# A delta-rule attention with an MLP on one core: constants and a weight request moved within the opening, chunk 0's output turned earlier

## The chip, the cores and the metric

The kernel runs on one core of one Trainium2 chip. The time is device microseconds of one launch. Engines in the profile: PE is TensorE's matrix multiply (PEld its weight loads), DVE is VectorE, ACT is ScalarE, POOL is GpSimd, SP is SyncE, which only issues transfers. Each engine runs its own queue in order, and the queues meet only at semaphores.

## The reference

Attention by the delta rule over 4 batches x 8 heads, 768 steps, head size 48, and then an MLP on all 3072 tokens (384 to 2048 to 384 with a tanh GELU).

```python
k_n = k / (np.linalg.norm(k, axis=-1, keepdims=True) + 1e-06)
state = np.zeros((B, H, D, D), dtype=np.float32)
for t in range(S):
    y[:, :, t] = np.einsum('bhd,bhde->bhe', q[:, :, t], state)
    v_old = np.einsum('bhde,bhd->bhe', state, kt)
    state = state + bt[:, :, :, None] * np.einsum('bhd,bhe->bhde', kt, vt - v_old)
...
h = x @ w_in
g = 0.5 * h * (1.0 + np.tanh(c * (h + 0.044715 * h * h * h)))
return (g @ w_out).astype(np.float32)
```

## The kernel before

The 768 steps are cut into 12 chunks of 64. A chunk covers all 32 heads; it is worked as two units of 16 heads each (unit u = 2 x chunk + 0 or 1). Inputs are float32, the working copies bf16. What one chunk goes through:

- **norms** (L497 to L503): squares of k on ACT (`sq`), their sums on DVE (`sum`), the root (`pow`, on ACT for the first three chunks), `eps` and the reciprocal `inv`.
- **prep** (L531 to L586): `kn` multiplies k by the inverse norm into the tile `tok`, `qb` casts q beside it; PE turns them (`Tk`, `Tq`, or `T` for both, L540), an eviction `kTk`, `kTq` or `kT` follows; Gram products `GD`, `GQ` or `G` (L564); `dn` evicts the k-k half, `wq` the masked k-q half.
- **leaf** (L633 to L669): `F` folds the 8 x 8 blocks on the diagonal, `lp`, `x0` and six pairs `xm`, `xa` on DVE solve them, `xb` scales by beta.
- **scale** (L599 to L623): `xe` or `xec` spread that into the tile `zt`; `KZ` and `GM` are products on PE, `kz` and `lw` their evictions. `lw` holds the lower triangle of the chunk's matrix.
- **invert** (L682 to L717): `X10`, `X11` copy its diagonal into `bd`, and two doublings (`A4`, `rt4`, `B4`, `bde4..`, then `A5`, `rt5`, `B5`, `be5..`) give the inverse.
- **chain** (L752 to L812): from chunk to chunk, `V`, `K`, `R`, `U`, `Un`, the new state `S` and `Sn`, the output `O` and `On`; the output is turned for the MLP by `X` on PE and the eviction `xT`, or by a transposing transfer.
- **mlp** (L824 to L844): 16 up-projections `up`, GELU in four parts on ACT, 8 groups of `down` matmuls, `Z` evicts, `out` stores.

A name such as `GM.4` is GM of unit 4, `X.0` is X of chunk 0. Nothing is scheduled at run time or by a planner: the text `ORDER` lists every operation once, in one global order. `kn.2:d` means kn of unit 2 on DVE (a is ACT, g POOL, s SP), no letter means PE, and `@6` is the first PSUM bank of the result. From this list each engine gets its own queue. `Flow.add` records what each operation reads and writes, and `Flow.emit` sets a semaphore wait wherever an operation needs one on another engine, or a bank whose last reader is on another engine. So an operation that waits holds all that stands behind it in its engine's queue.

Constants come in the same list. Some names: `tmpl`, a template of -1 diagonals; `sel`, `rows`, `blk`, `own`, masks for the leaf; `rowz` clears `rows` and `rows1` (L382) fills it; `two` (L380), `unit`, `muq`, `mlw`, `low1` more masks; `pad` and `bdz` clear borders of `tok` and `bd`; `triwq`, `trilw` preset `wq`, `lw` from the template; `ladj4`, `ladj5` (L416, L418) preset the tiles `rl`; `first` (L400) sets the first column of `xl`; `wz` clears the operand of filler matmuls (`fill`, L426). `betaN` evict the turned beta; `w1.0`, `w1.1` (L481) request the two halves of W1 on POOL's queue, `w2` those of W2. The loads of q, k and v (L472) are on SP's queue, the first few of k on ACT's.

The lines that set one of the waits that matter below, the bank of a product:

```python
            if o.alloc:
                b = self.at[o.alloc[0]]
                for y in range(b, b + o.alloc[1]):
                    o.bankdeps.update(last[y])
```

Of the kernel before, what the change touches and what calls it, by code (L numbers as in the profile page):

```python
# [15 lines left out]

ORDER = """
bdz3:d tmplz:g k0x1.10:a k1.01:s tmpl0:g tmpl1:g bdz5:d k0x1.00:a beta11:s blk1:g one:g pad2:g pad0:d pad5:d ident:g trilw0:d beta01:s beta10:a bdz4:d
ident2:g bdz0:g k0x1.01:s k0x1.11:a mmlw:d identf:d blk2:g k1.00:s beta00:a blk3:g k0x0.00:a k1.10:s half:g own:g triwq4:g trilw1:a k1.11:s sel:d
q0.10:s k0x0.10:a unit:d betaT1@0 triwq0:g q0.01:s mmuq:d mln0:g tabS:a bdz2:g sq.0b:a k2.00:s pad4:g mwp0:g betaN101:d k0x0.11:a betaT0@6 sum.0b:d  # L20
rowz:g q0.00:s betaN100:d mln1:g pow.0b:a q0.11:s eps.0b:d pad1:g inv.0b:d betaN001:d sq.1:a kn.1:g q2.11:s k0x0.01:a sum.1:d k2.10:s muq0:g Tk.1@1
muq1:g ladj4.0:a k2.01:s betaN011:d pow.1:a betaN110:d eps.1:g pad3:d k2.11:s inv.1:d triwq1:d betaN010:d low1:d kn.2:d v0.10:s kn.3:d qb.1:a Tk.2@7
v0.01:s qb.0:g Tk.3@5 kTk.2:d q2.01:s rows1:g Tq.1@4 sq.0a:a betaN111:d kTk.1:d q2.10:s kTq.1:d kTk.3:a sum.0a:d q2.00:s GD.3@4 betaH1:d pow.0a:a
Tq.0@7 sq.2:a eps.0a:d rpad0:g v1.00:s inv.0a:d GD.2@2 betaN000:d GD.1@0 dn.3:a kn.0:g betaL1:d q1.01:s betaH0:d betaS1@6 dn.2:a sum.2:d low2:g
q1.00:s dn.1:a Tk.0@4 first0:d F.1@2 kTq.0:d pow.2:a q1.10:s eps.2:g kTk.0:d trilw2:g q1.11:s GQ.1@0 lp.1:d GD.0@4 betaL0:d x0.1:d L.1@7 q3.01:s
dn.0:a two:d inv.2:d GQ.0@2 wz:d knc.2:g xm1.1:d qbc.2:a F.0@4 k3.00:s wq.0:d xa1.1:d q3.10:s betaS0@5 xm2.1:d xa2.1:d betaS3@2 w1.0:g lp.0:d k3.11:s
betaC0:a xm3.1:d ladj5.1:d L.0@3 triwq2:a ladj4.1:d T.5@4 v0.00:s x0.0:d wqa.1:a xm1.0:d first1:g xa1.0:d kT.5:a qb.3:g xa3.1:d xm2.0:d v0.11:s
xa2.0:d trilw3:g Tq.3@0 xm4.1:d xm3.0:d betaC1:a xa3.0:d qb.2:g xa4.1:d xm5.1:d xm4.0:d T.4@6 xa4.0:d xa5.1:d betaS2@1 xm5.0:d xm6.1:d kT.4:a xa6.1:d
xa5.0:d Tq.2@4 kTq.3:d xb.1:g xm6.0:d triwq5:g xa6.0:d betaC2:a xb.0:d G.5@6 w1.1:g kTq.2:a xe.1:d G.4@0 dn.4:a v2.11:s xe.0:d KZ.1@4 kz.1:a wq.4:d
mwp1:g dn.5:a GM.1@4 xec.1:d KZ.0@0 ladj5.0:a F.2@3 wqa.5:a betaC3:a lw.1:d kz.0:a lp.2:d bdz1:d L.2@3 k3.01:s GM.0@4 x0.2:d X10.1:g KZ.2@6 lw.0:d  # L30
KZ.3@0 kz.3:a X11.1:g kz.2:a xm1.2:d GM.3@0 xa1.2:d rpad1:g A4.1@2 X11.0:g lw.3:d X10.0:g rt4.1:d k3.10:s xm2.2:d A4.0@1 X11.3:g xa2.2:d v1.01:s
B4.1@2 xm3.2:d xa3.2:d rt4.0:d q3.11:s GQ.2@6 GM.2@4 vb.0:a xm4.2:d vb.1:g wq.2:d k4.11:s B4.0@1 bde40.1:a triwq3:g lw.2:d V.0@6 X10.3:g k4.01:s
bde41.1:a bde40.0:a k4.00:s wqb.1:g xa4.2:d A4.3@2 xm5.2:d bde41.0:a A5.1@0 k4.10:s rt4.3:d GQ.3@4 R.0:a rt5.1:d A5.0@1 X11.2:g B4.3@2 v1.10:s rt5.0:d
B5.1@0 bde40.3:a xa5.2:d q3.00:s B5.0@7 X10.2:g xm6.2:d fill115@1 xa6.2:d be50.1:d be50.0:a v1.11:s wq.3:d xb.2:g be51.1:a A4.2@3 sq.3:a w2.0:g
be51.0:d v2.01:s xe.4:d U.0@0 bde41.3:d KZ.4@4 Un.0:a w2.1:g rt4.2:d kz.4:a O.0@6 sum.3:d A5.3@4 On.0:a S.0@2 rt5.3:d GM.4@0 sq.4:a xe.5:d X.0@6
B4.2@7 lw.4:d Sn.0:a fill85@4 KZ.5@4 xT.0:a sum.4:d X11.4:g bde40.2:a up4.0@2 kz.5:d pow.3:g up0.0@0 bde41.2:a up1.0 X10.4:d tabG:a up2.0 up12.0@6
qbc.3:d up3.0 A5.2@4 up13.0 rt5.2:d gelu0.0:a up5.0 up6.0 GM.5@4 eps.3:d inv.3:d knc.3:d up7.0 up14.0 A4.4@0 lw.5:d up15.0 turn.7:s B5.2@1 gelu3.0:a
rt4.4:d up8.0@4 X11.5:g up9.0 gelu1.0:a B5.3@0 vbc.1:g down00.0@6 be50.3:d up10.0 be51.3:a X10.5:d pow.4:g be50.2:a up11.0 V.1@2 gelu2.0:a T.6@0
v2.00:s A4.5@7 kT.6:d v2.10:s be51.2:a K.1 down01.0 R.1:a rt4.5:d q5.00:s G.6@4 k5.10:s B4.5@7 dn.6:a B4.4@2 xi4.5:d U.1@0 bde40.4:a down02.0 k5.00:s
wq.6:d bdc40.5:g Un.1:a down03.0 k5.01:s bde41.4:d bdc41.5:g eps.4:g A5.5@1 k5.11:s Z0.0:d wqb.5:g S.1@4 Q.1@2 q4.11:s Sn.1:d G.7@6 O.1 vbc.2:g  # L40
q4.01:s A5.4@0 rt5.5:d On.1:a down10.0@5 inv.4:d q4.10:s dn.7:d kn.9:g down11.0 rt5.4:d q4.00:s wq.7:d F.3@1 q5.01:s B5.4@4 lp.3:d V.2@2 sq.5:a x0.3:d
v3.10:s L.3@1 B5.5@0 xm1.3:d X.1@6 be50.4:a v3.01:s be50.5:a xa1.3:d K.2 be51.5:a xm2.3:d down12.0 be51.4:a xa2.3:d q5.11:s xT.1:d R.2:a down13.0
xm3.3:d q5.10:s xa3.3:d xm4.3:d qbc.4:g up0.1@2 xa4.3:d Z1.0:a up12.1@6 xm5.3:d xa5.3:d up1.1 kn.8:g xm6.3:d sum.5:d turn.9:s U.2@4 up13.1 Un.2:a
up14.1 xa6.3:d pow.5:g xb.3:d up15.1 xec.3:d Q.2@0 gelu3.1:a S.2@4 turn.8:s O.2 up2.1 Sn.2:d On.2:a up3.1 up8.1@6 gelu0.1:a qb.11:d up9.1 KZ.6@0
eps.5:d KZ.7@4 inv.5:d kz.6:a up10.1 kn.11:d up11.1 kz.7:a up4.1@0 kn.10:g turn.11:s qb.10:a GM.6@2 gelu2.1:a G.9@4 lw.6:d up5.1 up6.1 dn.9:a up7.1
T.10@6 X11.6:g v3.11:s wq.9:d gelu1.1:a down10.1@7 kT.10:d k6.10:s GM.7@4 X10.6:d G.8@2 k6.00:s G.10@0 lw.7:d dn.8:a down11.1 v3.00:s dn.10:a F.4@6
X10.7:d k6.11:s wqa.10:a down12.1 X11.7:g lp.4:d wq.8:d k6.01:s A4.6@4 G.11@0 x0.4:d q6.00:s rt4.6:d L.4@5 dn.11:a A4.7@6 X.2@2 xm1.4:d v4.00:s
# [856 lines left out]
```

## Time and profile before

| | |
|---|---|
| median of 3 runs | 254.64 us (254.4 to 255.61) |
| span of the profiled execution | 254.7 us (no other time of it is given; it lies within 0.1 of the median) |
| PE busy | 226.0 us, 89% |
| DVE busy | 185.8 us, 73% |
| ACT busy | 157.4 us, 62% |
| POOL busy | 130.1 us, 51% |
| first up-projection (L824) | starts at 49.94 us |

Rows of the profile read so: start, duration (us), engine, line, operation, out<-in by the program's names without buffer numbers, the shape, and a count where several were merged; in brackets the idle time of that engine just before, and what ended it. A row of stages gives a stretch, its length, then for PE, PEld, DVE, ACT and POOL the busy time and number of instructions, the granted TensorE clock (1.00 is full), the share of the transfer engines that was busy and GB/s.

### The profile page before, as it was taken

Reading aid. Unit: us, or ns where it says so; the run is one execution under the profiler, and the core shown is the slowest. Engines: PE = TensorE matmul, PEld = TensorE weight load, DVE = VectorE, ACT = ScalarE, POOL = GpSimd, SP = SyncE. Lnnn points to the kernel's source line nnn. Section 1 sums busy time; section 2 is a strip of 40 time slices with the busy share of each in tenths; the row PEclk is TensorE's granted clock in tenths of the full one; section 3 lists DMA queues with packets and bytes.
Section 4 is the critical chain, followed back from the end, with each engine's and each line's share of the span. In section 5 each row is a group of like instructions: output and inputs, shape, how many; then the busy total and the mean of one; then the engine's idle time right before and its main releaser. Section 6 shows DMA issues by size and latency. Waiting matters only on the chain.

```text
span 254.7 us, 12256 instructions
## 1 busy us (share of the span) xinstructions
PE 226.0 (89%) x5500; PEld 178.3 (70%) x5502; DVE 185.8 (73%) x445; ACT 157.4 (62%) x244; POOL 130.1 (51%) x159
## 2 busy tenths in 40 slices
...
GB/s 103 165 144 118 184 162 95 165 127 117 128 130 105 112 126 124 135 165 147 119 146 167 100 36 131 147 153 130 56 93 167 62 49 4 33 68 64 3 93 62
DMA packets 104532, 28.25 MB, mean 111 GB/s; under 512 B 98592, under 2 KB 103712, under 8 KB 104480
## 3 DMA queue, kind: packets, MB, share of 16 engines
...
q8 instruction: 43, 0.70, 1.2%
q10 hardware_dynamic: 2400, 0.54, 1.1%
...
HBM read 20.64 MB, written 4.72 MB: 100 GB/s over the span
## 4 chain that ended last, share of the span: by engine, by line
PE 73%; DVE 15%; ACT 4%; DMA 2%; ACTq 2%; issue 2%; SPq 1%; POOL 0%
PE ps L835 24%; PE ps L824 22%; PE ps L692 5%; PE ps L620 3%; PE ps L752 3%; PE ps L773 2%; DMA vraw<-in_v_dram 2%; PE ps L697 2%; PE ps L564 2%; DVE lw L623 2%; DVE xl L658 2%; PE ps L633 2%; PE ps L759 2%; DVE ps L655 2%; PE ps L609 1%
## 5 line engine op out<-in xcount | busy, mean ns | idle before, releaser
L824 PE MATMUL ps<-xT,W 128*128 128x256 bf16 x576 | 76.8, 277 | 0.4 <-DVE xl L658 0.4
L835 PE MATMUL ps<-W,gT 128*128 128x384 bf16 x384 | 72.7, 326 | 0.0
L828 ACT ACTIVATE gT<-ps 128x1024 bf16<-128x1024 f32 x48 | 48.4, 1022 | 26.4 <-PE ps L824 25.8
L824 PEld LDWEIGHTS ps<-xT,W 128*128 128x128 bf16 x576 | 52.2, 99 | 9.3 <-DVE xl L658 0.5
L835 PEld LDWEIGHTS ps<-W,gT 128*128 128x128 bf16 x384 | 34.0, 97 | 18.2
L682 POOL TENSOR_SCALAR_AFFINE_SELECT bd<-lw 64x512 bf16<-64x512 bf16 x34 | 22.6, 667 | 37.7 <-DVE lw L623 28.6
L704 DVE TENSOR_TENSOR rl<-ps,two 128x384 bf16<-128x384 f32 (+1 forms) x48 | 22.9, 484 | 9.7 <-PE ps L692 9.5
L623 DVE CAST_PREDICATED lw<-mlw,ps 128x832 bf16<-128x832 uint16 x24 | 24.3, 1018 | 6.8 <-PE ps L620 6.5
L499 POOL TENSOR_TENSOR nrm<-nrm,half 128x16 f32<-128x16 f32 x9 | 26.6, 2956 | 2.8 <-DVE nrm L497 2.7
L343 ACT ACTIVATE bd<-ps 32x256 bf16<-32x256 f32 (+1 forms) x40 | 16.8, 428 | 8.2 <-PE ps L692 4.4
L692 PEld LDWEIGHTS ps<-lw,bd 128*128 128x128 bf16 x384 | 15.5, 98 | 4.2 <-POOL bd L682 1.2
L692 PE MATMUL ps<-lw,bd 128*128 128x32 bf16 (+1 forms) x384 | 17.2, 183 | 1.2 <-POOL bd L682 1.1
L658 DVE TENSOR_TENSOR xl<-ps,xl 128x96 bf16<-128x96 f32 (+4 forms) x72 | 16.0, 228 | 2.0
L655 DVE TENSOR_TENSOR ps<-ps,xl 128x64 f32<-128x64 f32 (+5 forms) x72 | 15.6, 221 | 2.0 <-PE ps L649 0.5
L343 ACT ACTIVATE ob<-ps 128x384 f32<-128x384 f32 x17 | 8.3, 490 | 14.0 <-PE ps L835 14.0
L722 POOL COPY bd<-xi 64x256 f32<-64x256 f32 x20 | 8.0, 401 | 16.4 <-ACT xi L343 8.5
L540 PE MATMUL ps<-ident,tok 128*128 128x128 bf16 x80 | 7.8, 246 | 8.1 <-POOL tok L531 3.8
L531 POOL TENSOR_TENSOR tok<-kraw,nrm 128x384 bf16<-128x384 f32 x9 | 8.5, 945 | 12.7 <-DVE bsb L349 5.6
L349 ACT ACTIVATE kT<-ps 128x512 bf16<-128x512 f32 x18 | 10.4, 596 | 6.4 <-PE ps L609 6.4
L343 ACT ACTIVATE dn<-ps 128x512 bf16<-128x512 f32 x18 | 10.4, 593 | 5.3 <-PE ps L564 5.3
L620 PE MATMUL ps<-kT 48*64 48x56 bf16 (+1 forms) x768 | 11.1, 196 | 2.8 <-ACT kT L349 1.4
L599 POOL TENSOR_TENSOR zt<-xb,blk 128x2048 bf16<-128x2048 bf16 x3 | 10.9, 3642 | 4.1 <-DVE xb L669 3.9
...
## 6 DMA issues: line engine op xcount, KB each, us to landing
...
kraw<-in_k_dram ACTq DMA_DIRECT2D x7, 48.0 KB, 3.3
...
```

Of the source, the lines that this page charges most:

```text
L343: return e.activation(out, in_, ACT.Copy) if e is nc.scalar else e.tensor_copy(out, in_)
L499: if e is nc.scalar else e.tensor_tensor(nr[:, 1, hx], nr[:, 0, hx], half[:, hx], ALU.pow), reads=[nrn, "half"] + ["one"] * (c < ROOTS),
L620: ins = e.matmul(P(ps("GM"))[hf(a), o_ + c0:o_ + c1], kT[s][r, y, g, hf(a)], kT[s][r, z, g, C * a + c0:C * a + c1])
L623: A(("dve",), op("lw"), lambda e, P: e.copy_predicated(lw[m][:, :, 0:LW - LB], mlw[:, :, :].rearrange("p w t -> p (w t)")[:, 16:16 + LW - ...
L655: A(("dve",), f"xm{m}.{c}", lambda e, P, m=m, w=w, part=part: e.tensor_tensor(part(P), P(f"L.{c}")[:, off[m]:off[m] + 2 * H * w].rearrange ...
L658: A(("dve",), f"xa{m}.{c}", lambda e, P, m=m, part=part: e.tensor_tensor(xl[y][:, :, m + 1:LB], part(P), xl[y][:, :, m + 1:LB], ALU.add), ...
L682: A(("pool", "dve"), op(f"X1{a}"), lambda e, P, src=lw[m][hf(a), :, LW - C:LW], dst=bd[b_][hf(a), :, hf(a)], a=a: e.affine_select(out=dst, ...
L692: ins = e.matmul(P(name)[:, C * h + c0:C * h + c1], bd[b_][:, h, :], rhs[:, h, :])
L704: A(("dve",), op(f"rt{i}"), lambda e, P, i=i, c0=c0, c1=c1, r_=r_: e.tensor_tensor(r_[:, 0:H, c0:c1], P(ps(f"A{i}")).rearrange("p (h t) -> ...
L824: ins = e.matmul(P(ph)[:, 256 * f:256 * f + 256].rearrange("p (x t) -> p x t", x=2), W1[:, j, 128 * (i + f):128 * (i + f) + 128], x_[:, :, ...
L828: A(("act",), f"gelu{i // 4}.{c}", lambda e, P, i=i, ph=ph: e.activation(g_[:, i:i + 4, :], P(ph).rearrange("p (f t) -> p f t", f=4), ACT. ...
L835: ins = e.matmul(P(po)[:, 0:DM], g_[:, f, 128 * b:128 * b + 128], W2[:, f, :], start=(f == 0), stop=(f == FC - 1))
```

## The change

Only `ORDER` changes; no operation is added, removed or given to another engine, and SP's queue stays word for word. What moves, engine by engine:

- DVE: `two`, `wz`, `ladj5.1`, `ladj4.1` to just ahead of `sel`; `first0` behind `unit`; `bdz1` behind `muq`'s clear; `triwq1`, `pad3`, `low1` ahead of `sum.0b`; `inv.1`, `kn.2`, `kn.3` ahead of three `betaN`; `be51.0` ahead of `wq.3`.
- POOL: `rowz` and `rows1` from 10 and 16 places later to behind `triwq0`; `triwq4` from ahead of `triwq0` to behind `qb.0`; the request `w1.0` from ahead of `first1` to behind `qb.2`.
- PE: `X.0` ahead of `GM.4`; `up4.0` behind `up0.0` and `up1.0`.
- ACT: `xT.0` ahead of `Sn.0`.

Two of the lines that differ, in the old and the new form:

```diff
-muq1:g ladj4.0:a k2.01:s betaN011:d pow.1:a betaN110:d eps.1:g pad3:d k2.11:s inv.1:d triwq1:d betaN010:d low1:d kn.2:d v0.10:s kn.3:d qb.1:a Tk.2@7
+inv.0b:d betaN001:d sq.1:a kn.1:g q2.11:s k0x0.01:a sum.1:d k2.10:s muq0:g Tk.1@1 muq1:g ladj4.0:a k2.01:s pow.1:a eps.1:g k2.11:s inv.1:d kn.2:d
...
-be51.0:d v2.01:s xe.4:d U.0@0 bde41.3:d KZ.4@4 Un.0:a w2.1:g rt4.2:d kz.4:a O.0@6 sum.3:d A5.3@4 On.0:a S.0@2 rt5.3:d GM.4@0 sq.4:a xe.5:d X.0@6
+be51.0:d wq.3:d v2.01:s xe.4:d U.0@0 bde41.3:d KZ.4@4 Un.0:a w2.1:g rt4.2:d kz.4:a O.0@6 sum.3:d A5.3@4 On.0:a S.0@2 rt5.3:d X.0@6 GM.4@0 sq.4:a
```

DVE where chunk 1's k is normalised, before; the row with two multiplies is kn.2 and kn.3, the rows on `bsb` are betaN, the row on kT2 is kTk.2:

```order
L497 TENSOR_REDUCE nrm1<-sq1 128x16
L349 TENSOR_SCALAR bsb0<-ps 64x2x4
L349 TENSOR_SCALAR bsb0<-ps 64x22x4
L403 MEMSET tok0 128x16x8
L503 RECIPROCAL nrm1<-nrm1 128x16
L343 COPY wq1<-tmpl0 128x512
L349 TENSOR_SCALAR bsb0<-ps 64x2x4
L396 MEMSET low0 128x1
L531 TENSOR_TENSOR tok0<-kraw1,nrm1 128x8x48 x2
L343 COPY kT2<-ps 128x512
```

And after:

```order
L497 TENSOR_REDUCE nrm1<-sq1 128x16
L503 RECIPROCAL nrm1<-nrm1 128x16
L531 TENSOR_TENSOR tok0<-kraw1,nrm1 128x8x48 x2
L349 TENSOR_SCALAR bsb0<-ps 64x2x4
L349 TENSOR_SCALAR bsb0<-ps 64x22x4
L349 TENSOR_SCALAR bsb0<-ps 64x2x4
L343 COPY kT2<-ps 128x512
```

Three constants have left, and the multiplies follow the reciprocal at once, with the three betaN behind them. POOL from `own` on, before (the two copies are triwq4 and triwq0, L381 is rowz, the last row kn.1):

```order
L390 TENSOR_TENSOR own0<-blk0 128x64
L411 COPY wq4<-tmpl0 128x256
L411 COPY wq0<-tmpl0 128x256
L372 AFFINE_SELECT mlw0<-mlw0 64x64
L421 MEMSET bd2 128x512
L403 MEMSET tok0 128x16x8
L374 AFFINE_SELECT mlw0<-mlw0 64x64
L381 MEMSET rows0 128x512
L372 AFFINE_SELECT mlw0<-mlw0 64x64
L403 MEMSET tok0 128x16x8
L531 TENSOR_TENSOR tok0<-kraw0,nrm0 128x8x48
```

And after:

```order
L390 TENSOR_TENSOR own0<-blk0 128x64
L411 COPY wq0<-tmpl0 128x256
L381 MEMSET rows0 128x512
L382 AFFINE_SELECT rows0<-rows0 128x1024
L372 AFFINE_SELECT mlw0<-mlw0 64x64
L421 MEMSET bd2 128x512
L403 MEMSET tok0 128x16x8
L374 AFFINE_SELECT mlw0<-mlw0 64x64
L372 AFFINE_SELECT mlw0<-mlw0 64x64
L403 MEMSET tok0 128x16x8
L531 TENSOR_TENSOR tok0<-kraw0,nrm0 128x8x48
```

rows1 (L382), which stood behind qb.0, is now ahead of the masks on `mlw` and of kn.1 (L531), and triwq4 is gone from here. PE at chunk 0's output, before (L782 is S.0, the rows on kT4 are GM.4, L807 is X.0, L609 KZ.5, L824 the first ups):

```order
L620 MATMUL ps<-kT4 64x48 x4
L807 MATMUL ps<-ident0,xo0 128x128 x6
L692 MATMUL ps<-rl0_0,bd2 128x64 x8
L426 MATMUL ps<-wz0 128x512
L609 MATMUL ps<-zt0,tok0 64x64 x16
L824 MATMUL ps<-xT0,W10 128x256 x18
```

And after:

```order
L782 MATMUL ps<-us0,tok0 64x48 x32
L807 MATMUL ps<-ident0,xo0 128x128 x6
L620 MATMUL ps<-kT4 64x56 x4
L620 MATMUL ps<-kT4 64x48 x4
L620 MATMUL ps<-kT4 64x56 x4
```

Before, X.0 followed the last part of GM.4; now it follows S.0, and GM.4 comes behind it.

54 lines of the change are left out of this document (27 added, 27 removed).

## The prediction

> **What bounds the kernel now.** I read the busy time by stage first, then the chain that ended last, then the instructions of VectorE in the opening 50 us, and last the clock in steps of 3.41 us. Stages (columns: span, then busy us of each engine with its instructions, then the granted TensorE clock, the DMA share, GB/s):
>
> ```profile
> 0.00:9.00 9.00, 1.46 (x12) 1.35 (x12) 4.32 (x12) 4.13 (x5) 7.05 (x26) 1.00 0.69 122
> 9.00:50.00 41.00, 26.02 (x777) 22.05 (x780) 38.35 (x107) 26.41 (x49) 22.01 (x37) 0.83 0.87 145
> 60.00:190.00 130.00, 127.91 (x3440) 101.50 (x3437) 109.38 (x253) 90.92 (x143) 78.43 (x76) 1.00 0.71 123
> ```
>
> The reader is to see two kernels in one. From 60 to 190 us PE is busy 127.91 of 130 us, so nothing but PE work counts there. From 9 to 50 us it is DVE, 38.35 of 41 us, and the chain runs nearly all on DVE there; before 9 us DVE has 4.68 us idle. Whatever leaves DVE between 9 and 50 us can bring the first up-projection forward, and from there on every stage is relative to the one before, so the same amount should reach the end. The change touches only the head, so the sum is about when the first up-projection (L824) starts.
>
> **rows1 and kn.2 (the largest term).** All engines in order of time, about 12 to 16 us:
>
> ```profile
> 12.14 0.25 DVE L503 RECIPROCAL nrm<-nrm 128x16 f32<-128x16 f32 x1
> 12.17 0.50 POOL L343 CAST tok<-qraw 128x384 bf16<-128x384 f32 x1
> 12.31 0.51 DVE L343 COPY wq<-tmpl 128x512 bf16<-128x512 bf16 x1
> 12.63 2.05 POOL L382 TENSOR_SCALAR_AFFINE_SELECT rows<-rows 128x1024 bf16<-128x1024 bf16 x1
> 12.85 0.17 DVE L349 TENSOR_SCALAR bsb<-ps 64x8 f32<-64x8 f32 x1
> 13.06 1.96 DVE L531 TENSOR_TENSOR tok<-kraw,nrm 128x384 bf16<-128x384 f32 x1
> ...
> 14.95 0.54 DVE L531 TENSOR_TENSOR tok<-kraw,nrm 128x384 bf16<-128x384 f32 x1
> ...
> 15.72 0.42 DVE L343 COPY kT<-ps 128x512 bf16<-128x512 bf16 x1 [0.23 <-PE ps L540]
> ```
>
> kn.2 takes 1.96 us and its twin kn.3, of the same shape, 0.54. kn.2 ends at 15.02, 0.34 us after POOL's rows1 ends at 14.68: it was held by it. The change moves rows1 ahead by some 7 us. Then inv.1 still ends at 12.39 (it waits for POOL's eps.1), and kn.2 comes right behind. POOL at that time is in qb.0, until 12.67, and then in triwq4, for which this row stands (same form):
>
> ```profile
> 28.82 0.39 POOL L411 COPY wq<-tmpl 128x256 f32<-128x256 f32 x1
> ```
>
> If both hold kn.2 it ends at 12.67 + 0.39 + 0.34 = 13.40; kn.3 follows 0.47 later as before (15.49 - 15.02), at 13.87. The three betaN evictions that now stand behind it cost 3 x 0.17: 14.38. Then comes kTk.2, for which PE's transposes of kn.2's tile would be done at 13.40 + 0.70 = 14.10 (0.70 is 15.72 - 15.02 today). So kTk.2 starts at 14.38 and not 15.72: **1.34**. Bounds: nothing held, 12.39 + 0.54 + 0.47 + 0.51 = 13.91, a gain of 1.8; kn.3 held by triwq4 too, 0.95. I take the middle case, since a held multiply is what the trace shows. What follows kTk.2 (the norms of chunk 0, kn.0 on POOL, the folds) hangs on DVE and moves with it; the loads these need have landed before.
>
> **What is pushed in ahead of 9 us.** DVE's idle time there takes two, wz, the two ladj, first0, bdz1, triwq1, pad3 and low1. None of it is on a path if it is done by 9.00, when sum.0b can start, which waits for ACT's square:
>
> ```profile
> 4.62 1.38 DVE L391 TENSOR_TENSOR sel<-ident,own 128x1024 bf16<-128x1024 bf16 x1 [1.22 <-POOL own L390]
> ...
> 9.00 0.55 DVE L497 TENSOR_REDUCE nrm<-sq 128x8 f32<-128x384 f32 x1 [1.40 <-ACT sq L495]
> ```
>
> But rows1 now runs here. This pair shows what a small cast on DVE does beside a POOL multiply; the cast has 16 elements a partition and ends with the POOL instruction, at 19.36 against 19.33:
>
> ```profile
> 18.45 0.88 POOL L531 TENSOR_TENSOR tok<-kraw,nrm 128x384 bf16<-128x384 f32 x1 [3.69 <-DVE bsb L349]
> ...
> 18.56 0.80 DVE L447 CAST bhl<-bsb 128x16 bf16<-128x16 f32 x1
> ```
>
> sel ends at 6.00; rows1, held by it as kn.2 was held by rows1, runs to about 8.05, and first0, a cast of the same kind, waits for it. Behind first0 stand mmuq, bdz1 (0.48, row below), betaN101, triwq1 (0.51 above), pad3 and low1, by these rows about 1.25 us: sum.0b at 9.3, **0.3 lost**, and all behind it, since ACT's next square and POOL's eps.1 move too. Not held, it costs nothing; held longer, as by a rows1 that starts late, 0.5.
>
> Here a rule of the Trainium skill speaks against the change. The page "SBUF — State Buffer", section "SBUF: two separate sides", says that VectorE and GpSimd share one port pair as an exclusive lock for a whole instruction, between a GpSimd instruction that reads SBUF and a VectorE one with two SBUF inputs or in a two-port mode. The rows above agree (1.96 against 0.54 us). By that rule rows1 does not become free by being moved: it is paid where it next meets such an instruction, here sel and first0. With the rule the sum is the one below; without any hold it would be 0.3 better.
>
> On POOL itself kn.1 waited 1.86 us idle for inv.0b, which ended at 10.24; rows1 comes in ahead of it and triwq4 goes out:
>
> ```profile
> 10.32 0.83 POOL L531 TENSOR_TENSOR tok<-kraw,nrm 128x384 bf16<-128x384 f32 x1 [1.86 <-DVE bsb L349]
> ```
>
> 2.05 - 0.39 = 1.66 more POOL work fits into 1.86, so kn.1 is not late by this alone.
>
> **The W1 request, ladj, wz.**
>
> ```profile
> 23.45 1.01 POOL L481 DMA_DIRECT2D W<-in_moe_w_in_dram  x1
> ...
> 23.92 0.94 DVE L418 TENSOR_SCALAR rl<-tmpl 128x256 bf16<-128x256 bf16 x2
> ...
> 24.78 0.56 DVE L640 SCALAR_TENSOR_TENSOR xl<-lp,unit 128x112 bf16<-128x112 bf16 x1
> ```
>
> With the two ladj gone x0.0 can start where they did: 24.78 - 23.92 = **0.86**. It could be held by POOL's casts there, as today (0.56); bounds 0.5 and 1.2. From x0.0 to the first block product the chain stays on DVE, so the gain holds. wz, two and first0 also leave, at 20 to 22 us, but wq.0 behind them waits for the Gram product GQ.0 on PE, so their own time is mostly covered: I put it at 0.05, at most 0.1. The W1 request goes behind three POOL instructions; POOL is through with them before xb.1, which waited for DVE. W1 was requested 26 us before the first L824 uses it (23.45 against 49.94): no cost, and no gain by itself. The loads on SP's queue are in the same order; each is asked for as early or earlier.
>
> **bdz1, be51.0.**
>
> ```profile
> 33.71 0.48 DVE L421 MEMSET bd<- 128x512 f32 x1
> ...
> 43.52 0.67 DVE L571 CAST_PREDICATED wq<-muq,ps 128x512 bf16<-128x512 uint16 x1
> 44.22 0.42 DVE L343 CAST bd<-ps 32x256 bf16<-32x256 f32 x1
> ```
>
> bdz1 is followed by x0.2 and then by lw.0, which waits for PE's product GM.0; that product stands behind L.2, which waits for lp.2 and not for bdz1. Without bdz1 DVE waits 0.48 longer for PE: no gain. be51.0 ahead of wq.3 lets U.0 start about 0.3 earlier, but the eviction kz.4, which stands ahead of On.0 on ACT, waits for xe.4 on DVE, behind the same sum of work; I take 0 and keep 0.3 as the upper bound.
>
> **X.0 ahead of GM.4, xT.0 ahead of Sn.0.**
>
> ```profile
> 47.44 0.60 PE L620 MATMUL ps<-kT 48*64 48x56 bf16 x32
> 47.97 0.82 PE L807 MATMUL ps<-ident,xo 128*128 128x128 bf16 x6
> 48.59 0.64 PE L692 MATMUL ps<-rl,bd 128*128 128x64 bf16 x8
> 49.58 0.43 PE L609 MATMUL ps<-zt,tok 64*64 64x64 bf16 x16 [0.36 <-DVE lw L623]
> 49.94 3.81 PE L824 MATMUL ps<-xT,W 128*128 128x256 bf16 x18
> ```
>
> and on ACT:
>
> ```profile
> 48.83 0.81 ACT L343 ACTIVATE xT<-ps 128x768 bf16<-128x768 bf16 x1
> ```
>
> xT.0 ends at 49.64, but PE has the same four pieces to do in either order and is through with the last, KZ.5, at 50.01. An earlier xT.0 only waits longer: 0. The other side of it: GM.4 and with it lw.4 on DVE come some 0.7 us later, and lw.4 frees the banks of up0.0, which is now the first up. By the rows that is ready at 49.9, just when PE gets there. X.0 may also wait for On.0, up to 0.3. I take 0 with a bound of 0.3 lost.
>
> **Sum.** 1.34 - 0.3 + 0.86 + 0.05 = 1.95. The profiled span is 254.67 us, 0.03 above the median of the runs, so the same sum holds against either: 252.7; I say **252.8**. By the bounds alone the gain lies between 0.65 and 3.4.
>
> **The clock, and the rivals.**
>
> ```profile
> 46.57:49.98 3.41, 3.00 (x109) 2.71 (x105) 3.41 (x5) 3.34 (x6) 0.62 (x1) 0.50 1.22 179
> 49.98:53.39 3.41, 3.41 (x21) 2.43 (x18) 1.57 (x4) 2.19 (x4) 2.99 (x2) 0.50 1.31 204
> 53.39:56.81 3.42, 3.42 (x78) 2.92 (x77) 2.77 (x6) 1.21 (x2) 0.00 (x0) 1.00 0.50 78
> ```
>
> The granted clock changes only at these edges, 3.41 us apart: half through the first ups, full after one stretch in which PE was busy throughout. A stretch at half clock costs PE half of it, 1.7 us. In this run the ups began at 49.94 and the first full stretch began at 49.98, the best that can be.
>
> (a) *Late clock.* With ups at about 48.0 the edges may fall so that the first full stretch begins up to 3.4 us later: up to 1.7 us lost, and 253.7 to 254.5. For it speaks that the runs before spread over 1.2 us; against it, that an edge may as well fall well. 0.15. The Trainium skill ("TensorE: Matmul & The Clock Gate", Part 1) calls the window free-running, not reset when a kernel starts, which is this rival; the trace agrees with its 3413 ns, and no single run can show that it is not reset.
>
> (b) *The stalls only move.* rows1 and the new DVE work cost 0.5 ahead of 9 us, kn.2 and kn.3 are both held (0.95), x0.0 gives 0.5: gain 0.95, 253.7. Chance 0.15.
>
> (c) *No effect:* the head waits for loads that are asked for no earlier, and the gains on DVE turn into waits there. 254.6. Against it, DVE's idle time from 9 to 50 us is 2.65 of 41, almost none of it on DMA. 0.03.
>
> (d) *Slower.* PE is less dense ahead of the ups: X.0 waits for On.0, up0.0 for lw.4. If a gap falls into the first stretch of ups, and again into the second, the clock stays half for two stretches more: 3.4 us against 1.95, 256.1. One stretch only takes the gain; the second decides. 0.04.
>
> **How the numbers follow.** 0.63 for the forecast and what is better than it (251.5 to 253.3 is its own range), and 0.15, 0.15, 0.03 and 0.04 as given. This kernel's times tell a difference of about 0.5%, 1.3 us, from none: faster is below 253.4, slower above 255.9. (a) and (b) lie mostly just above 253.4; a small part of them below it: faster 0.66, same 0.30, slower 0.04. The range, 251.5 to 254.5, takes in (a) and (b) and leaves out (c), (d) and the best bound.
>
> **What the profile after would show.** Right: kn.2 near 0.9 us or less; kTk.2 at 14.2 to 14.8; L418 ahead of sel; x0.0 some 2 us earlier; sum.0b at 9.0 to 9.3; the first L824 at 47.5 to 48.3, and idle PE no larger than now from there on. Wrong: sum.0b past 9.5; kn.2 still near 2 us; DVE waiting for DMA between 14 and 24 us; or the first L824 early but its half-clock stretch longer than 3.8 us. A wait in the middle, where SP's loads set the pace, could also take the gain back after the head.

## The result and the profile after

| | before | after |
|---|---|---|
| median of 22 runs | 254.33 us (253.06 to 257.1) | 252.85 us (251.82 to 256.74) |
| ratio | | 0.9944, interval 0.9922 to 0.9965 |
| span of the profiled execution | 254.7 us | 250.0 us |
| kTk.2 / x0.0 / first L824 start at | 15.72 / 24.78 / 49.94 us | 14.44 / 22.33 / 47.59 us |

The change makes the kernel 0.6% faster. The forecast was 252.8 us, 251.5 to 254.5. A second comparison, with 12 runs of the changed kernel, gave the ratio 0.9943 (0.991 to 0.9975). The ratios leave out runs more than 1.5% above the fastest run of the same kernel, two of the 22 after; for two kernels below a single fast run makes that three of 12 and two of six, so those two ratios come out low.

The stages of the profile after, with the columns of the rows shown before:

```profile
0.00:9.00 9.00, 1.46 (x12) 1.35 (x12) 7.04 (x19) 4.13 (x5) 7.56 (x24) 1.00 0.70 124
9.00:50.00 41.00, 28.09 (x805) 23.40 (x808) 37.01 (x105) 28.52 (x52) 23.06 (x41) 0.83 0.95 151
60.00:190.00 130.00, 128.57 (x3394) 102.24 (x3393) 109.28 (x260) 91.47 (x142) 79.00 (x77) 1.00 0.70 124
```

DVE's work went into the first 9 us (4.32 to 7.04 us), and from 9 to 50 us its idle time grew from 2.65 to 3.99 us: part of what left DVE came back as waits. In order of time, rows1, first0 and sum.0b; then inv.1 to kTk.2 (the two multiplies kn.2 and kn.3 in one row, the three betaN in one row):

```profile
5.82 2.33 POOL L382 TENSOR_SCALAR_AFFINE_SELECT rows<-rows 128x1024 bf16<-128x1024 bf16 x1 [0.15 <-POOL rows L381]
...
6.61 1.59 DVE L400 CAST xl<-unit 128x16 bf16<-128x16 f32 x1
...
9.21 0.54 DVE L497 TENSOR_REDUCE nrm<-sq 128x8 f32<-128x384 f32 x1
...
12.34 0.25 DVE L503 RECIPROCAL nrm<-nrm 128x16 f32<-128x16 f32 x1 [0.62 <-POOL nrm L501]
12.38 0.50 POOL L343 CAST tok<-qraw 128x384 bf16<-128x384 f32 x1
...
12.63 1.33 DVE L531 TENSOR_TENSOR tok<-kraw,nrm 128x384 bf16<-128x384 f32 x2
12.83 0.72 POOL L411 COPY wq<-tmpl 128x256 f32<-128x256 f32 x1
...
13.99 0.42 DVE L349 TENSOR_SCALAR bsb<-ps 64x8 f32<-64x8 f32 x3
...
14.44 0.42 DVE L343 COPY kT<-ps 128x512 bf16<-128x512 bf16 x1
```

The cast first0 has 16 elements a partition and ends at 8.20 with rows1 (8.15); the copy triwq1 and the rest follow it, and sum.0b is 0.21 late. kn.2 and kn.3 take 1.33 us together instead of 1.96 and 0.54, and kTk.2 is 1.28 us earlier.

Next, chunk 0's first block product. L.0 on PE (L649) waits for lp.0, and xm1.0 on DVE for L.0:

```profile
22.33 0.33 DVE L640 SCALAR_TENSOR_TENSOR xl<-lp,unit 128x112 bf16<-128x112 bf16 x1
...
22.34 0.38 PE L649 MATMUL ps<-lp,rows 128*128 128x96 bf16 x6 [0.18 <-DVE lp L637]
...
23.23 0.27 DVE L655 TENSOR_TENSOR ps<-ps,xl 128x96 f32<-128x96 f32 x1 [0.57 <-PE ps L540]
```

In the profile before, xm1.0 followed x0.0 at once:

```profile
25.38 0.27 DVE L655 TENSOR_TENSOR ps<-ps,xl 128x96 f32<-128x96 f32 x1
```

x0.0 is 2.45 us earlier, xm1.0 (the last row of the profile after) only 2.15: 0.57 us of idle DVE ahead of it is new. The profile names the transposes queued on PE behind L.0, but by the reads and writes in the kernel's list xm1.0 needs only x0.0 and L.0. Last, the end of the head: be51.0, xe.4, lw.4, and the first up.

```profile
41.86 0.42 DVE L343 CAST bd<-ps 32x256 bf16<-32x256 f32 x1 [0.41 <-ACT bd L343]
...
42.91 0.68 DVE L602 TENSOR_TENSOR zt<-xb,blk 128x1024 bf16<-128x1024 bf16 x1
...
46.43 1.02 DVE L623 CAST_PREDICATED lw<-mlw,ps 128x832 bf16<-128x832 uint16 x1
...
47.59 1.58 PE L824 MATMUL ps<-xT,W 128*128 128x256 bf16 x13 [0.48 <-ACT st L343]
```

xe.4 and lw.4 in the profile before:

```profile
44.67 0.69 DVE L602 TENSOR_TENSOR zt<-xb,blk 128x1024 bf16<-128x1024 bf16 x1
...
48.19 1.02 DVE L623 CAST_PREDICATED lw<-mlw,ps 128x832 bf16<-128x832 uint16 x1
```

Ahead of be51.0 DVE is idle for 0.41 us, waiting for ACT; up to there the gain on DVE was 2.14, behind it xe.4 and lw.4 are 1.76 earlier. PE waits 0.48 us ahead of the first up: Sn.0, which the profile names, ends at 47.51, and lw.4, whose banks up0.0 takes, at 47.45. By the kernel's list up0.0 waits for lw.4 and for xT.0, done at 46.8, and not for Sn.0.

**The two spans are not alike in clock.** All stretches of 3.41 us from 43.36 us on are at full clock here, while in the profile before two of them, with the first ups in them, were at half. In the runs after, the time is the span and 1.7 to 2.0 us more, and 19 of the 20 runs compared have one of two mean clocks: 7 have 0.972 to 0.973, median 252.37 us, and 12 have 0.963 to 0.966, median 253.70. The two groups overlap: five of the 12 lie between 252.36 and 252.89 us. The profile after is of the first kind. A repeat of the changed kernel, shown below, is of the second: two half stretches under the first ups, and one fewer ahead of them. So the 4.7 us between the two spans are not all the head's.

### The profile page after: what moved, and what is told of

The parts are those of the page before. It is cut to its first block, busy times and chain, and to the rows that moved or that the text cites. A ratio compares the mean times of both kernels' runs of the same rounds, so it can differ in the third digit from the quotient of the medians.

```text
span 250.0 us, 12256 instructions
## 1 busy us (share of the span) xinstructions
PE 223.8 (90%) x5500; PEld 176.3 (71%) x5502; DVE 185.1 (74%) x445; ACT 157.4 (63%) x244; POOL 130.1 (52%) x159
## 4 chain that ended last, share of the span: by engine, by line
PE 73%; DVE 19%; POOL 4%; issue 2%; ACT 1%; ACTq 0%; POOLq 0%
PE ps L835 26%; PE ps L824 21%; PE ps L692 5%; PE ps L752 3%; PE ps L620 3%; PE ps L697 2%; PE ps L564 2%; PE ps L759 2%; DVE lw L623 2%; PE ps L773 2%; DVE xl L658 2%; PE ps L633 2%; DVE ps L655 2%; DVE nrm L497 1%; PE ps L609 1%
## 5 line engine op out<-in xcount | busy, mean ns | idle before, releaser
L824 PE MATMUL ps<-xT,W 128*128 128x256 bf16 x576 | 75.0, 273 | 0.9 <-ACT st L343 0.5
L824 PEld LDWEIGHTS ps<-xT,W 128*128 128x128 bf16 x576 | 51.3, 97 | 8.9 <-DVE lw L623 0.7
L682 POOL TENSOR_SCALAR_AFFINE_SELECT bd<-lw 64x512 bf16<-64x512 bf16 x34 | 22.8, 672 | 35.7 <-DVE lw L623 30.1
L531 POOL TENSOR_TENSOR tok<-kraw,nrm 128x384 bf16<-128x384 f32 x9 | 8.5, 950 | 10.5 <-PE ps L782 4.5
```

The source lines that it names most:

```text
L682: A(("pool", "dve"), op(f"X1{a}"), lambda e, P, src=lw[m][hf(a), :, LW - C:LW], dst=bd[b_][hf(a), :, hf(a)], a=a: e.affine_select(out=dst, ...
L824: ins = e.matmul(P(ph)[:, 256 * f:256 * f + 256].rearrange("p (x t) -> p x t", x=2), W1[:, j, 128 * (i + f):128 * (i + f) + 128], x_[:, :, ...
```

## Experiments

All edits are moves of words in `ORDER`; the diffs show the words around each place.

**The kernel before, once more** (no edit).

> The kernel before, unchanged, once more. In the runs of the changed kernel the time is the span plus 1.8 us, and they fall in two groups by their mean granted clock: 0.973 (median 252.4 us) and 0.965 (median 253.8 us), one stretch of 3.41 us at half clock apart. Theory 'clock on top': the profiled execution of before that the prediction used (span 254.7) was a late-clock one, worth about 256.5 us; most executions of before have spans of 252.0 to 253.0, and they too fall in groups by the clock about 1.4 us apart; compared group by group the change is worth about 2 us. The first L824 starts at 49.9 within 0.3 in this profile too, whatever the clock does. Theory 'the head swings': the first L824 itself comes 1 us or more earlier or later from run to run (loads), and the groups by clock do not show.

Time 254.28 us, ratio 0.9999 (0.9974 to 1.0023); span 252.3, clock 0.972, time of that execution 254.19. kTk.2 at 15.74, x0.0 at 24.78, and the first up again at 49.94:

```profile
49.94 1.16 PE L824 MATMUL ps<-xT,W 128*128 128x256 bf16 x8
```

The ups had one stretch at half clock instead of two: up8.0 came at 55.55 and not at 56.75. The profiled execution of before with span 254.7 therefore stood for a time near 256.5 us, not for the median. Far behind the change, between 139 and 147 us, it lost another 1.4 us against this one, and got 0.4 of it back by 169 us. That it was one of the slower executions, by its clock among other things, is borne out. That the runs of before fall in groups by the clock is not: of these 12, eight have a mean clock of 0.970 to 0.973, one 0.960, and three 0.980, with times of 253.55, 254.19 and 255.81 us. And a low clock is rare in this kernel: 15 of its 91 runs with a clock on record lie at 0.967 or below, against 14 of the 22 runs of the changed kernel above.

**rows1 back, the rest of the change kept.**

```diff
-triwq0:g rowz:g rows1:g q0.01:s
+triwq0:g q0.01:s
...
-sum.0b:d q0.00:s
+sum.0b:d rowz:g q0.00:s
...
-q2.01:s Tq.1@4
+q2.01:s rows1:g Tq.1@4
```

> The changed kernel with rowz and rows1 alone back at their old places on POOL (rowz behind kn.1's predecessors, rows1 behind qb.0 and triwq4). Theory 'what counts is that kn.2 does not meet rows1': kn.2 now follows inv.1 at once and is over before rows1 begins at about 13.5, so kn.2 stays at 0.6 to 0.7 us and kn.3 below 0.8; the betaN and kTk.2 read PSUM and are not held; first0 falls from 1.59 to 0.2 us, sum.0b comes at 9.0, and kTk.2 at 14.2 to 14.3, 0.2 earlier than in the changed kernel; the first L824 0 to 0.2 earlier. Theory of the prediction 'the early place of rows1 earns the 1.3 us': kn.3 or kTk.2 is held to the end of rows1, kTk.2 comes at 15.4 to 15.8 and the first L824 at about 48.7.

Ratio 0.9951 (0.9919 to 0.9983), as the changed kernel. DVE and POOL in order of time (betaN in one row again):

```profile
12.43 1.33 DVE L531 TENSOR_TENSOR tok<-kraw,nrm 128x384 bf16<-128x384 f32 x2
13.78 0.42 DVE L349 TENSOR_SCALAR bsb<-ps 64x8 f32<-64x8 f32 x3
14.23 0.42 DVE L343 COPY kT<-ps 128x512 bf16<-128x512 bf16 x1
...
13.31 2.31 POOL L382 TENSOR_SCALAR_AFFINE_SELECT rows<-rows 128x1024 bf16<-128x1024 bf16 x1
```

kTk.2 comes at 14.23, 0.21 earlier than in the profile after, and the instructions that read PSUM beside rows1 take what they always take. With rows1 ahead it can come at 14.23 too: the repeat of the changed kernel, shown below, has that. So the early place of rows1 is not what earns the 1.3 us; that kn.2 and kn.3 are done before it starts is enough. The 0.2 did not get far: wq.0 waits for the Gram product GQ.0 and came at 20.68, as in the changed kernel (20.70), and the first up, at half clock, at 48.0.

**rows1 alone, on the kernel before.**

```diff
-triwq0:g q0.01:s
+triwq0:g rowz:g rows1:g q0.01:s
```

(and both words out of their old places, the fifth and the 13th behind triwq0 in POOL's queue)

> The kernel before with rowz and rows1 alone moved ahead, to behind triwq0; DVE's order is that of before. Theory 'all that counts is that rows1 and kn.2 do not meet': kn.2 starts at 13.06 as before and takes 0.55 to 0.65, kTk.2 comes at 14.3 to 14.5, 1.2 to 1.4 earlier than in the kernel before, and the first L824 at 48.6 to 48.8; sum.0b stays at 9.00. Rival 'moving kn.2 ahead of triwq1, low1 and betaN earns it': kTk.2 stays later than 15.0. Rival 'the early place costs': sum.0b later than 9.1.

Ratio 0.9979 (0.9951 to 1.0007). POOL and DVE in order of time:

```profile
4.78 1.73 POOL L411 COPY wq<-tmpl 128x256 f32<-128x256 f32 x2
...
12.48 0.26 POOL L501 TENSOR_SCALAR nrm<-nrm 128x16 f32<-128x16 f32 x1 [0.16 <-POOL muq L376]
...
12.77 0.25 DVE L503 RECIPROCAL nrm<-nrm 128x16 f32<-128x16 f32 x1 [0.64 <-POOL nrm L501]
...
13.76 0.55 DVE L531 TENSOR_TENSOR tok<-kraw,nrm 128x384 bf16<-128x384 f32 x1
...
15.02 0.42 DVE L343 COPY kT<-ps 128x512 bf16<-128x512 bf16 x1 [0.24 <-PE ps L540]
```

kn.2 is free (0.55), as the first theory says, but kTk.2 gains only 0.70 of 1.34. That just meets the rival's "later than 15.0", though not for its reason: eps.1 is late on POOL, and inv.1 with it, by 0.63. sum.0b stays at 9.00, so the early place did not cost there. POOL had triwq4 and triwq0 there, the second of them held by sel (1.40 us of the 1.73), then rows1, and its 1.86 us of slack ahead of kn.1 was gone. In the changed kernel triwq4 has left and triwq0 starts before sel. What kTk.2 gained arrives: be51.0 is 0.71 and the first up, at 49.21, 0.73 earlier than before, the latter at full clock here and at half in the profile before.

**first0 back behind sum.2.**

```diff
-unit:d first0:d betaT1@0
+unit:d betaT1@0
...
-Tk.0@4 F.1@2
+Tk.0@4 first0:d F.1@2
```

> The changed kernel with first0 alone back behind sum.2, where POOL has left rows1 behind. Theory 'first0 is held by rows1 and delays sum.0b': first0 takes about 0.2 us there, sum.0b starts at 9.0 instead of 9.23 and kTk.2 at 14.2; kn.2 and x0.0 come 0.2 earlier, the first L824 at 47.4. Rival 'the lock only moves on': another of the small instructions behind it (betaN, mmuq, bdz1) is held to the end of rows1 at 8.15 in its place, and sum.0b stays at 9.2.

Ratio 0.9968 (0.9942 to 0.9995). DVE, then POOL:

```profile
7.53 0.76 DVE L343 COPY wq<-tmpl 128x512 bf16<-128x512 bf16 x1
...
9.00 0.55 DVE L497 TENSOR_REDUCE nrm<-sq 128x8 f32<-128x384 f32 x1 [0.55 <-ACT sq L495]
...
12.42 1.53 DVE L531 TENSOR_TENSOR tok<-kraw,nrm 128x384 bf16<-128x384 f32 x2
...
12.37 0.50 POOL L343 CAST tok<-qraw 128x384 bf16<-128x384 f32 x1 [0.27 <-DMA qraw<-in_q_dram]
12.82 0.72 POOL L411 COPY wq<-tmpl 128x256 f32<-128x256 f32 x1
```

The hold does move on, to triwq1 (0.76 against 0.41), but within DVE's slack, so sum.0b starts at 9.00 as the first theory says. Yet kTk.2 stays at 14.43 and the first up at 47.6: in this run qb.0 waits for its load, triwq4 behind it ends when it did, and kn.3 ends 0.41 after triwq4 (13.95 and 13.54; with rows1 back 13.75 and 13.35). The 0.2 won ahead of 9 us was lost again at that load; with rows1 back, where qb.0 started at 12.17, it lasted to kTk.2.

**The W1 request back; and, in another kernel, the two ladj back.**

```diff
-betaS3@2 lp.0:d
+betaS3@2 w1.0:g lp.0:d
```

> The changed kernel with the W1 request alone back ahead of first1, where it is issued at about 21.5 to 22.5 us. Theory of the prediction 'the request holds small DVE work beside it, its place costs the loads nothing': one DVE instruction beside it (lp.0, xm3.1 or x0.0) takes 0.3 to 0.6 us longer; since xm1.0 waits 0.57 us for L.0 behind x0.0 anyway, xm1.0 comes 0 to 0.3 later and the first L824 at 47.6 to 47.9. Rival 'the request is free for DVE': all DVE durations there stay as they are within 0.05 and the first L824 at 47.6. Rival 'an earlier W1 helps': the ups or what is ahead of them start earlier than 47.5.

```diff
-xm3.1:d L.0@3 triwq2:a T.5@4
+xm3.1:d ladj5.1:d L.0@3 triwq2:a ladj4.1:d T.5@4
```

> The changed kernel with ladj5.1 and ladj4.1 alone back ahead of x0.0, the W1 request staying late. Theory 'their 0.94 us was the W1 request beside them': the pair costs 0.2 to 0.35 us here, x0.0 comes that much later, and xm1.0, which waits for L.0, not at all: first L824 at 47.6. Theory 'their 0.94 us was their own or another hold': the pair costs 0.8 to 0.95 again, x0.0 starts at 23.2, xm1.0 0.3 later and the first L824 at 47.9. In neither case does the 0.86 that the prediction counted reach the first L824 whole, since L.0 bounds xm1.0.

One execution each (253.59 and 253.76 us; clock 0.971). With the request back, DVE beside it:

```profile
22.28 0.33 DVE L640 SCALAR_TENSOR_TENSOR xl<-lp,unit 128x112 bf16<-128x112 bf16 x1
23.55 0.27 DVE L655 TENSOR_TENSOR ps<-ps,xl 128x96 f32<-128x96 f32 x1 [0.94 <-PE ps L649]
```

The request, 21.77 to 22.78 on POOL, holds nothing, as the second theory says: x0.0 has its 0.33. xm1.0 waits longer because L.0 itself is later on PE (22.55) and takes 0.48 us instead of 0.38: PE's transposes start 106 ns apart up to 29.03 us in this run, and 56 ns apart from 19.46 to 29.70 us in the profile after. With the ladj back, DVE and the copy on POOL beside it:

```profile
22.55 0.68 DVE L418 TENSOR_SCALAR rl<-tmpl 128x256 bf16<-128x256 bf16 x2
23.15 0.62 DVE L640 SCALAR_TENSOR_TENSOR xl<-lp,unit 128x112 bf16<-128x112 bf16 x1
...
22.62 0.57 POOL L411 COPY lw<-tmpl 128x448 f32<-128x448 f32 x1
```

Without the request the pair still takes 0.68 us, against 0.47 where the change puts it, and ends at 23.23 with POOL's copy (23.19); x0.0 is held next, to 23.77. So the pair's 0.94 us in the kernel before need not have been the request's doing: POOL's other work holds it as well. xm1.0 starts 1.58 us after lp.0 in both runs, with the pair (23.82 and 22.24) and without it (23.55 and 21.97), so with PE this slow the pair costs it nothing here; in the profile after it is 1.21 us. The first ups come at 48.79 and 49.10, later than every theory had them, but with PE slow up to 29 us and at half clock again from 46.10 and 46.34 us on they can't be set beside 47.59.

**X.0, xT.0 and up4.0 back.**

```diff
-rt5.3:d X.0@6 GM.4@0 sq.4:a
-xe.5:d B4.2@7 lw.4:d xT.0:a Sn.0:a fill85@4 KZ.5@4 sum.4:d X11.4:g bde40.2:a kz.5:d
+rt5.3:d GM.4@0 sq.4:a
+xe.5:d X.0@6 B4.2@7 lw.4:d Sn.0:a fill85@4 KZ.5@4 xT.0:a sum.4:d X11.4:g bde40.2:a up4.0@2 kz.5:d
```

> The changed kernel with X.0, xT.0 and up4.0 alone back at their old places. Theory of the prediction 'worth nothing': PE has the same work ahead of the first up either way, the first L824 stays at 47.6 within 0.15. Rival 'worth a quarter': On.0 still comes at about 44.6, xT.0 shifts back behind Sn.0 and ends at 47.5, KZ.5 at 47.9 and the first L824 starts at 47.8 to 47.9. Rival 'it costs': with GM.4 first, lw.4 is 0.5 earlier and the first L824 comes at 47.2 to 47.3.

Ratio 0.9941 (0.9916 to 0.9966), span 250.3, all ups at full clock. The first up:

```profile
47.38 0.83 PE L824 MATMUL ps<-xT,W 128*128 128x256 bf16 x6 [0.63 <-ACT xT L343]
```

It starts 0.2 earlier and now waits for xT.0; of that, 0.13 is there at be51.0 already (41.73 against 41.86), and up8.0 is 0.13 earlier (53.63 against 53.77). PE is at full clock from 40.80 us on here, and from 43.36 in the profile after. As far as the two can be set side by side, the hoist is worth nothing, as predicted.

**be51.0 back behind wq.3, beside the changed kernel once more.**

```diff
-be51.0:d wq.3:d v2.01:s
+be51.0:d v2.01:s
...
-v1.11:s xb.2:g
+v1.11:s wq.3:d xb.2:g
```

> The changed kernel with wq.3 alone back ahead of be51.0. In the changed kernel DVE is idle for 0.41 us ahead of be51.0, which waits for ACT's be50.0, and lw.4, for which up0.0 then waits 0.48, hangs on DVE. Theory 'be51.0 ahead of wq.3 cost what it was to gain': that idle time closes, U.0 and On.0 come 0.1 to 0.3 later, but xe.4 and lw.4 0.3 to 0.4 earlier (lw.4 at 46.0 to 46.2 at full clock) and the first L824 at 47.2 to 47.4. Theory of the prediction 'no effect': lw.4 and the first L824 move by less than 0.1. Rival: On.0 and xT.0 bound the first up, which comes 0.2 later.

> The changed kernel once more, unchanged, beside the next three. Theory: DVE's part of the head repeats within 0.3 us (kTk.2 14.1 to 14.5, x0.0 22.2 to 22.5); what differs is the clock: with full clock ahead of the first ups be51.0 comes at 41.9 and the first L824 at 47.6, with half clock there (as in the run with the W1 request put back) be51.0 at 42.6 and the first L824 up to 48.8. Time 252.5 to 253.2. Rival 'the place in the program decides and not the clock': first L824 at 47.6 whatever the clock does.

Both profiles have half clock under the first ups. DVE of the changed kernel (be51.0, xe.4, lw.4), and then two of its stretches of 3.41 us:

```profile
41.92 0.42 DVE L343 CAST bd<-ps 32x256 bf16<-32x256 f32 x1 [0.41 <-ACT bd L343]
...
42.97 0.68 DVE L602 TENSOR_TENSOR zt<-xb,blk 128x1024 bf16<-128x1024 bf16 x1
...
47.04 1.02 DVE L623 CAST_PREDICATED lw<-mlw,ps 128x832 bf16<-128x832 uint16 x1 [0.47 <-PE ps L620]
```

```profile
45.00:48.41 3.41, 3.05 (x100) 2.51 (x97) 2.94 (x5) 3.07 (x6) 0.20 (x1) 0.50 1.26 187
48.41:51.83 3.42, 3.42 (x17) 2.43 (x16) 1.90 (x4) 2.09 (x4) 3.34 (x2) 0.50 1.28 185
```

and with wq.3 first (be51.0, xe.4, lw.4):

```profile
42.34 0.42 DVE L343 CAST bd<-ps 32x256 bf16<-32x256 f32 x1
42.78 0.69 DVE L602 TENSOR_TENSOR zt<-xb,blk 128x1024 bf16<-128x1024 bf16 x1
...
47.10 1.02 DVE L623 CAST_PREDICATED lw<-mlw,ps 128x832 bf16<-128x832 uint16 x1 [0.71 <-PE ps L620]
```

The idle 0.41 is gone, and xe.4 is 0.19 earlier although be50.1 ahead of it was 0.20 later in this run (41.30 against 41.10): the move had cost DVE 0.39. Whether that reaches the first up at full clock stays open; here lw.4 waits 0.71 for PE, which is at half clock, the first up comes at 48.30 instead of 48.24, and up8.0 is only 0.10 earlier (55.02 against 55.12).

The repeat of the changed kernel (253.59 us, ratio 0.9943) differs from the profile after in the opening. Its first0, sum.0b and kTk.2:

```profile
6.36 1.60 DVE L400 CAST xl<-unit 128x16 bf16<-128x16 f32 x1
...
9.00 0.55 DVE L497 TENSOR_REDUCE nrm<-sq 128x8 f32<-128x384 f32 x1
...
14.23 0.42 DVE L343 COPY kT<-ps 128x512 bf16<-128x512 bf16 x1
```

sel starts at 4.65 here and at 4.90 in the profile after. That 0.25 us is enough: first0 is held as long (1.60 us), but sum.0b is not late, and kTk.2 comes 0.21 earlier. Five more profiles with this order of rows1 and first0 have sel at 4.87 to 4.90 and sum.0b at 9.18 to 9.22. The 0.21 is gone at wq.0, which starts at 20.73 against 20.70; from there to xe.5 the two agree within 0.06 us.

The repeat also gives a price of the clock, from this one pair of profiles. Its first up comes at 48.24, up8.0 at 55.12 and not at 53.77: two half stretches cost 1.35 us, close to the distance between the two medians by clock (1.33). Against the profile of before, which had two half stretches under the ups too, the first up is 49.94 - 48.24 = 1.70 earlier and up8.0 56.75 - 55.12 = 1.63. The lead over that profile stays between 1.4 and 1.8 us up to 135 us.

The runs beside it, of both kernels, have their clocks on record. At a mean clock of 0.970 to 0.973 the changed kernel takes 252.31 us (median of five runs) and the kernel before 254.82 (14 runs); at 0.967 or below 253.65 (five) and 255.70 (three); above 0.973 it has one run of 253.32, and the kernel before four with a median of 253.53. So in the two larger groups the change is worth 2.5 and 2.0 us at the same clock, from few runs, while the medians of all runs differ by only 1.21: six of the 12 runs of the changed kernel have the lower clock, and three of the 21 of the kernel before.

**Four stalls that the profile after shows, in two versions, and one part of them alone.** The first puts rows1 back, lp.0 behind wq.0 with L.0 ahead of betaS3, up4.0 ahead of up0.0, and pow.3 ahead of X11.4 on POOL. The part is the last two moves alone. The second version:

```diff
-unit:d first0:d betaT1@0
+unit:d betaT1@0
...
-eps.1:g k2.11:s inv.1:d kn.2:d
+eps.1:g k2.11:s betaN011:d betaN110:d inv.1:d kn.2:d
...
-qb.0:g triwq4:g Tk.3@5 betaN011:d betaN110:d betaN010:d
+qb.0:g Tk.3@5 betaN010:d
...
-dn.3:a kn.0:g
+dn.3:a kn.0:g triwq4:g
...
-wq.0:d xa1.1:d q3.10:s betaS0@5 xm2.1:d
+wq.0:d lp.0:d xa1.1:d q3.10:s betaS0@5 L.0@3 xm2.1:d
...
-sum.3:d A5.3@4
+sum.3:d pow.3:g A5.3@4
...
-up0.0@0 bde41.2:a up1.0 up4.0@2 X10.4:d
+up4.0@2 up0.0@0 bde41.2:a up1.0 X10.4:d
```

(first0 goes behind Tk.0 again, lp.0, L.0 and pow.3 out of their old places)

> The changed kernel with what the traces point to: rowz and rows1 back at their old places (behind kn.2 and kn.3, as in the run before: 0.2 earlier up to lp.1), lp.0 directly behind wq.0 and its product L.0 ahead of betaS3 (against the 0.57 us that xm1.0 waits for L.0), up4.0 again ahead of up0.0 (against the 0.48 us that PE waits for lw.4 ahead of the first up), and pow.3 ahead of X11.4 on POOL, right behind sum.3 (against the wait of eps.3, knc.3 and lw.5 for it). Theory 'these waits are the bound': xm1.0 at 22.7 to 22.9, be50.1 0.4 earlier, the first L824 at 46.8 to 47.1, eps.3 at about 49.5 to 50, up8.0 0.5 to 0.9 earlier, and a time 0.7 to 0.9 us below the changed kernel: ratio to the kernel before 0.990 to 0.993. Rival 'the waits only move': xm1.0 held by another operation, pow.3 holding lw.4 or xe.5 on DVE, first L824 not before 47.4, time as the changed kernel (0.994 to 0.996).

> The changed kernel with two moves behind the head: up4.0 again ahead of up0.0, and pow.3 on POOL ahead of X11.4, right behind sum.3. Theory 'what bounds the changed kernel now lies here': at full clock the first up starts at 46.9 to 47.2 instead of 47.6, eps.3 follows rt5.2 at about 50 instead of 51.3, PE's gap of 0.41 ahead of up8.0 closes, and the time is 0.5 to 0.9 us below the changed kernel of the same call. Rival 'PE is the bound from the first up on, and the ups only move against each other': less than 0.3 us.

> The changed kernel with first0 behind sum.2, betaN011 and betaN110 back ahead of inv.1 (into the 0.62 us in which DVE waits there), triwq4 behind kn.0 (so that it does not hold kn.2 and kn.3), lp.0 behind wq.0 and L.0 ahead of betaS3, and the two moves behind the head of the kernel before it in this call. Theory 'each stall on DVE ahead of 24 us counts': kn.2 and kn.3 take 0.55 each, kTk.2 comes at 13.6 to 13.8, GQ.0 and with it wq.0 about 0.4 earlier than in the changed kernel, xm1.0 at 22.6 to 22.9, the first up 0.3 to 0.6 earlier than in the kernel before it in this call, time 1.0 to 1.5 us below the changed kernel. Rival 'PE takes it back': wq.0, which waits for GQ.0, and xm1.0, which waits for L.0, stay at 20.7 and 23.2, and the time is that of the kernel before it in this call.

| | median us | ratio to before | first up (at half clock), up8.0 |
|---|---|---|---|
| changed kernel, repeated | 253.59 | 0.9943 (0.991 to 0.9975) | 48.24, 55.12 |
| the last two moves alone | 252.71 | 0.9895 (0.9837 to 0.9952) | 48.13, 54.74 |
| first version | 251.57 | 0.9882 (0.9851 to 0.9914) | 48.13, 54.99 |
| second version | 251.64 | 0.9889 (0.9855 to 0.9924) | 47.54, 53.26 |

Both versions come out faster than the change, about 1.1% ahead of the kernel before. The second ran beside the repeat of the changed kernel, and its median is 1.95 us lower, though the two intervals touch; the first was run with the kernel before, but not with the changed one. For the second the trace shows what was won on DVE:

```profile
12.13 0.25 DVE L503 RECIPROCAL nrm<-nrm 128x16 f32<-128x16 f32 x1 [0.26 <-POOL nrm L501]
12.42 1.26 DVE L531 TENSOR_TENSOR tok<-kraw,nrm 128x384 bf16<-128x384 f32 x2
...
13.92 0.42 DVE L343 COPY kT<-ps 128x512 bf16<-128x512 bf16 x1
...
21.29 0.28 DVE L637 TENSOR_TENSOR lp<-ps,bsb 128x112 bf16<-128x112 f32 x1 [0.16 <-PE ps L633]
...
22.93 0.27 DVE L655 TENSOR_TENSOR ps<-ps,xl 128x96 f32<-128x96 f32 x1
```

The wait ahead of inv.1 shrinks from 0.62 to 0.26, kn.3 is no longer held (only kn.2 by qb.0), kTk.2 comes at 13.92 (13.6 to 13.8 expected), and xm1.0 waits for nothing. Of the 0.52 won at kTk.2, 0.30 is left at xm1.0, and the first up is 0.59 earlier than with the last two moves alone. At xe.5 it is only 0.21 (45.55 against 45.76); between the two lw.4 waits for PE, which is at half clock from 45.34 us in this run and from 44.35 in the other, so part of the 0.59 is the clock's. This run had one half stretch under its ups and the other two, so up8.0 can't be set side by side. The first version missed its expectation in the head: x0.0 took 0.56 us beside POOL's copy into `lw`, xm1.0 came at 23.17 and not 22.8. Its profile at half clock shows only 0.11 to 0.13 us at the ups, so where its median comes from is not shown, and whether the last two moves earn anything alone is left open by their interval. pow.3 did run at once (45.59 instead of 48.34), but eps.3 then waited behind rt5.2, for which PE at half clock was late.

## Why the prediction came out right

- **rows1 and kn.2, 1.34:** kTk.2 moved by 1.28 in the profile after and by 1.49 in the repeat. The sum had 1.34 less the 0.3 of sum.0b up to there, that is 1.04; with the 0.21 by which sum.0b was late added back, the term itself is 1.49 in both. So it was sized a little low, and the reason was half right. The hold is real, but "the change moves rows1 ahead" is not what frees kn.2: with rows1 in its old place the same DVE order gives 14.23, as in the repeat, and rows1 moved by itself gives 0.70, as POOL's queue makes inv.1 late. The step that was sound is "kn.2 comes right behind inv.1".
- **sum.0b, -0.3:** 0.21 late in the profile after, by first0 held for 1.59 us, as worked out, and on time in the repeat. The rule that was quoted there, on the port of VectorE and GpSimd ("SBUF — State Buffer", "SBUF: two separate sides", in the Trainium skill), fits these runs: rows1 was paid at first0, triwq1 or nowhere, by what stood beside it. first0 and triwq1 have one SBUF input each, and no run shows whether they are in the two-port mode that the rule names.
- **ladj, 0.86:** x0.0 moved by 2.45 against 1.59 at lp.0, the 0.86 to the digit; but 0.30 was handed back at once, since xm1.0 waits for L.0, which hangs on lp.0 and not on x0.0. The step "from x0.0 to the first block product the chain stays on DVE" is the one that failed. From lp.1 to lp.0 the profile after takes 2.43 us and the one before 2.73, where 0.05 was put down for wz, two and first0. The repeat takes 2.68, which is that 0.05; in the profile after PE came to its full rate earlier, at 19.46 us against 21.11 and 22.67, and GQ.0, for which wq.0 waits there, took 0.32 us instead of 0.43.
- **W1 request, bdz1, X.0 and xT.0, 0 each:** all three came out so, the W1 request as far as xm1.0 shows it. For bdz1 the reason was another: DVE does not wait longer ahead of lw.0 (0.39 us, before 0.46), but x0.2, where bdz1 stood, takes 0.71 us instead of 0.20 beside POOL's copy into `bd`, which now runs there.
- **be51.0, 0:** mis-sized. Its wait for ACT's be50.0 cost DVE 0.39. The prediction asked who waits for be51.0, not what be51.0 itself waits for. Whether the 0.39 reaches the first up is not shown.
- **The sum, 1.95:** with two half stretches under the ups on both sides the head gives 1.63 to 1.70; at the same mean clock the runs give 2.0 and 2.5 in the two larger groups; the medians of all runs differ by 1.48 and 1.21. The parts that missed pull against each other: kTk.2 came out ahead of the sum, the ladj 0.30 behind it and be51.0, on DVE, 0.39.
- **The base:** "The profiled span is 254.67 us, 0.03 above the median of the runs, so the same sum holds against either" was wrong. A span is 1.7 to 2.0 us below the time of its execution; the one shown had more half clock than most and its span happened to have the median's number. Since the sum was taken from a number that the median has too, the forecast did not suffer.
- **Luck in the number:** 252.8 was forecast and 252.85 came. The kernel before came out at 254.33 and not 254.64, and the gain at 1.48 and not 1.84; the two differences cancel.
- **The clock, rival (a):** given 0.15, and far more common: 20 of 34 runs of the changed kernel have the lower mean clock, against 15 of 91 of the kernel before. Of the 12 such runs in the table above, seven lie above 253.6 us, and all eight others below 253.3. That is part of why the medians differ by less than those groups do; why the change brings the lower clock more often is not shown. The free-running window ("TensorE: Matmul & The Clock Gate", Part 1, in the Trainium skill) agrees with two executions of one kernel, the profile after and the repeat, whose half-clock stretches ahead of the ups end at 43.36 and 41.59 us.
